# Cutting some output stores of an attention backward kernel at other rows

## The chip, the cores and the metric

The kernel runs on one core of one Trainium2 chip. A core has five engines with their own instruction streams: TensorE (PE, matmuls; its weight loads are listed as PEld), VectorE (DVE), ScalarE (ACT), GpSimd (POOL) and SyncE (SP). Data moves between the device memory (DRAM) and the on-chip buffer (SBUF) by DMA; 16 DMA engines serve the core. An instruction on SP or POOL only issues a transfer; the 16 DMA engines carry it out in packets, and each of the 16 adds one to a semaphore when its share of the transfer is done. Matmul results stand in PSUM, eight banks here.

The metric is the device time of one execution in microseconds (us), lower is better. The profile is one execution taken by the hardware profiler.

## The reference

Grouped-query attention with a softmax over all keys, its output, and the gradients for q, k and v:

```python
B, Hq, Hkv, Sq, Sk, D = 32, 32, 4, 4, 2048, 128      # all bfloat16
def _fwd_reference(q, k, v):
    k = jnp.repeat(k, Hq // Hkv, axis=1)
    v = jnp.repeat(v, Hq // Hkv, axis=1)
    scores = jnp.einsum("bhqd,bhkd->bhqk", q, k) * D ** -0.5
    return jnp.einsum("bhqk,bhkd->bhqd", _softmax(scores, axis=-1), v)

def reference(q, k, v, grad_out):
    out, vjp = jax.vjp(_fwd_reference, q, k, v)
    return (out, *vjp(grad_out))                      # out, dq, dk, dv
```

k and v are 64 MiB each and so are dk and dv; q, grad_out, out and dq are 1 MiB each. Nearly all traffic is k and v in, dk and dv out.

## The kernel before

One batch after another is worked through. The 32 query heads times 4 positions are the 128 rows of a tile; each of the 4 key heads has 2048 keys, held as 128 partitions of 16 keys (the index c, 16 blocks of 128). For a batch the kernel

- loads k and v, one transfer of 512 KB for each head (`LK`, line 154, and `LV`, line 160), issued from SP, into buffers `k_sb` (3 of them, each a whole batch) and `v_sb` (2),
- transposes k and v on PE, eight 128x128 blocks at a time (`KT`, `VT`, line 181), and copies the result out of PSUM on DVE (line 183),
- forms the scores (line 198), their maximum (line 211) and exponentials (line 222), the row sums (`NRM`), then transposes the exponentials (line 248) and gathers the output o (`O`, line 264),
- forms dP, dS and its transpose, and dq (`dQ`, line 264),
- forms dV and dK as eight outer products each (`outer`, matmuls in line 307, copies out of PSUM on ACT in line 311) into a 2 MB buffer out of a pool of four that dV and dK share.

The order on all engines is written out by hand (`HEAD`, `STEADY`, `TAIL`): one turn of the steady part mixes work of batch b with dK and dq of batch b-1 and with transposes of batch b+1, and issues the loads of batch b+2. A load of k waits until the dq of the batch that used the buffer has read it (three k buffers).

All results are stored from POOL's queue (`store`), in the order in which the program issues them: dq (line 294), dk and dv (line 337; the last batch in halves, line 323), o for two batches at a time (line 280). POOL also loads the next four batches' q and grad_out (line 142) every fourth batch. A store of dv or dk is one transfer of 128 partition rows by 4 heads of 4 KB, 2 MB in all, except:

- for every fourth batch (`b % 4 == 3`, b = 3, 7, ..., 27) dv goes out as heads 0 and 1 whole (128 rows) and heads 2 and 3 in a piece of 120 rows and a piece of 8 rows; the small piece goes first where b is 3, 11, 19 or 27, last where it is 7, 15 or 23,
- o of every second pair of batches (b = 7, 11, ..., 31) goes out as 52 rows and 76 rows (line 279).

Of the kernel before, what the change touches and what calls it, by code (L numbers as in the profile page):

```python
# [81 lines left out]
def kernel(ctx: ExitStack, tc: tile.TileContext, q, k, v, grad_out, out_0, out_1, out_2, out_3):  # L82
# [3 lines left out]
    P = 128  # L86
# [172 lines left out]
    def gathered(S, xt, kv):  # L259
        t = banks.take(1)  # L260
        ps = banks.ap(t)[:, 0, 0:D]
        for c in range(C):
            for h in range(NH):
                nc.tensor.matmul(  # L264
                    ps[G * h:G * h + G, :], lhsT=S[f"{xt}{c // 8}"][:, c % 8, G * h:G * h + G], rhs=S[kv][:, h, c, :],
                    start=(c == 0), stop=(c == C - 1), tile_position=(0, G * h),
                )
        return t, ps

    def O(b):  # L270
        S = st[b]
        t, ps = gathered(S, "et", "v")
        if b % 2 == 0:
            st["o"] = io_pool.tile([P, 2, D], BF16, name="o_sb")
        o_sb = st["o"][:, b % 2, :]
        nc.vector.tensor_scalar(out=o_sb, in0=ps, scalar1=S["rinv"][:], scalar2=None, op0=ALU.mult)
        banks.give(t)
        if b % 2:
            for r in (slice(0, 52), slice(52, P)) if b % 4 == 3 and b > 3 else (slice(0, P),):
                store.dma_start(out=o_f[b - 1:b + 1, r].rearrange("w p d -> p w d"), in_=st["o"][r])  # L280
        junk = sm_pool.tile([P, D], BF16, name="junk")
        S["delta"] = sm_pool.tile([P, 1], FP32, name="delta")
        nc.vector.tensor_tensor_reduce(
            out=junk[:], in0=o_sb, in1=S["do"], scale=1.0, scalar=0.0,
            op0=ALU.mult, op1=ALU.add, accum_out=S["delta"][:],
        )
# [9 lines left out]
    def outer(S, x, y, dst, name, i, b, copy):  # L296

        if name not in S:
            S[name + "left"] = 8
            S[name] = out_pool.tile([P, NH, C, D], BF16, name=name, tag="outp")  # L300
        t = banks.take(2)
        ps = banks.ap(t).rearrange("p a (j c d) -> p a j c d", j=2, c=2)
        for c in range(2):
            u = P * ((2 * i + c) % 8)
            for a in range(2):
                r = slice(2 * G * a, 2 * G * a + 2 * G)
                nc.tensor.matmul(  # L307
                    ps[:, a, :, c, :], lhsT=S[f"{x}{i // 4}"][r, u:u + P], rhs=S[y][r, :, :],
                    start=True, stop=True, tile_position=(2 * G * a, 0),
                )  # L310
        copy(  # L311
            out=S[name][:, :, 2 * i:2 * i + 2, :].rearrange("p h c d -> p h (c d)"),
            in_=banks.ap(t).rearrange("p a (j w) -> p (a j) w", j=2),
        )
        banks.give(t)
        S[name + "left"] -= 1
        if b == B - 1:

            half = f"{name}half{i // 4}"
            S[half] = S.get(half, 4) - 1  # L320
            if S[half] == 0:
                c = slice(8 * (i // 4), 8 * (i // 4) + 8)
                store.dma_start(
                    out=dst[b].rearrange("p h (c d) -> p h c d", d=D)[:, :, c, :].rearrange("p h c d -> p h (c d)"),
                    in_=S[name][:, :, c, :].rearrange("p h c d -> p h (c d)"),
                )
        elif S[name + "left"] == 0:
            o = S.pop(name)[:].rearrange("p h c d -> p h (c d)")
            parts = [(slice(0, P), slice(0, NH))]
            if name == "dv" and b % 4 == 3:  # L330

                cut = [(slice(0, 120), slice(2, 4)), (slice(120, P), slice(2, 4))]
                parts = [(slice(0, P), slice(0, 2))] + (cut if b % 8 == 7 else cut[::-1])
            for r, h in parts:
                store.dma_start(out=dst[b][r, h, :], in_=o[r, h])  # L337

    def dV(b, i, copy=nc.scalar.copy):
        outer(st[b], "e", "dop", dv_v, "dv", i, b, copy)  # L340

    def dK(b, i, copy=nc.scalar.copy):
        outer(st[b], "ds", "qp", dk_v, "dk", i, b, copy)

    def dP(b, i):
# [6 lines left out]
        banks.give(t)  # L352

    table = {"LK": LK, "LV": LV, "QDT": QDT, "O": O, "dQ": dQ, "NRM": NRM}
    for i, c in enumerate("ab"):
        for n, f in (("S", S_), ("EX", EX), ("dP", dP), ("ET", ET), ("dST", dST)):
# [16 lines left out]
    with tc.manual_schedule():  # L373

        for w in HEAD.split():
            w, b = w.split("@")
# [5 lines left out]
        for w in TAIL.split():  # L382
            w, b = w.split("@")
# [31 lines left out]
```

## Time and profile before

| | |
|---|---|
| median of 3 runs | 700.01 us (698.55 to 701.41) |
| the profiled execution | 700.94 us, its span 699.2 us |
| granted TensorE clock | 0.984 |
| busy share PE, DVE, ACT, POOL | 89%, 84%, 81%, 39% |
| moved by DMA | 274.45 MB, 393 GB/s over the span |

The span runs from the first to the last instruction that the profile shows. Busy shares are averages over the span; what bounds a stage is read from the chain of waits in that stage. In the profile the transfers issued from POOL stand under queue q0 (software dynamic), those from SP under q1 (hardware dynamic), and fetches of instructions under q8 and q14. An issue row gives the size of each transfer and the median time from its issue until the last of the 16 engines has reported its share.

### The profile page before, as it was taken

To read this page: it belongs to the slowest core of one execution; us is meant where nothing else is said; L and a number is where in the kernel's file an instruction comes from. 1 tells how busy PE (TensorE), PEld (TensorE's weight loads), DVE (VectorE), ACT (ScalarE), POOL (GpSimd) and SP (SyncE) were. 2 spreads that over 40 slices of the span, in tenths; PEclk is the share of its full clock that TensorE was granted. 3 is DMA by queue.
4 is the path that set the end of the run, shared out by engine and by line. 5 is a ranking of instruction groups with operands and counts; after the bars stand their busy time and mean duration, and the time that the engine had idled before them with its cause. 6 is when DMAs were issued, how large, how long until landed. Compare 5 with 4: busy or idle time off the path is not lost.

```text
span 699.2 us, 27997 instructions
## 1 busy us (share of the span) xinstructions
PE 625.1 (89%) x12352; PEld 452.5 (65%) x12352; DVE 586.6 (84%) x992; ACT 569.0 (81%) x673; POOL 270.8 (39%) x449
## 2 busy tenths in 40 slices
PE   6899999999988989989899888899988999888981
PEld 5577776667676666666566665667666667656661
DVE  5998999989887998879988888788888988878960
ACT  0698989889887888869798878887887988778994
POOL 1354342445342254432444423444333534314352
PEclk9999999999999999999999999999999999999996
DMA  8989999999999999999999999999999999999767
GB/s 341 394 305 411 417 415 416 416 412 417 413 415 414 413 416 409 414 405 403 417 395 410 412 407 398 381 413 413 418 399 371 414 412 416 397 385 375 291 253 276
DMA packets 74969, 274.45 MB, mean 393 GB/s; under 512 B 8033, under 2 KB 8061, under 8 KB 74848
## 3 DMA queue, kind: packets, MB, share of 16 engines
q0 software_dynamic: 36928, 138.17, 49.4%
q1 hardware_dynamic: 37920, 134.50, 48.6%
q8 instruction: 96, 1.57, 0.8%
q14 instruction: 25, 0.20, 0.1%
HBM read 136.31 MB, written 136.31 MB: 390 GB/s over the span
## 4 chain that ended last, share of the span: by engine, by line
DMA 48%; PE 41%; DVE 3%; issue 3%; ACT 2%; POOL 1%; SPq 0%; POOLq 0%; ACTq 0%; DVEq 0%
DMA k_sb<-in_k_dram 47%; PE banks L181 18%; PE banks L307 10%; PE banks L264 6%; PE banks L248 3%; PE banks L198 3%; ACT dv L311 1%; DVE kt L183 1%; DMA v_sb<-in_v_dram 1%; DVE ds L349 1%; DVE m L211 1%; DVE vt L183 0%; ACT dk L311 0%; PE banks L171 0%; POOL dop L231 0%
## 5 line engine op out<-in xcount | busy, mean ns | idle before, releaser
L311 ACT CAST dk<-banks 128x1024 bf16<-128x1024 f32 x256 | 251.0, 1027 | 44.0 <-PE banks L307 41.3
L311 ACT CAST dv<-banks 128x1024 bf16<-128x1024 f32 x256 | 245.7, 1028 | 46.2 <-PE banks L307 45.6
L183 DVE COPY kt<-banks 128x1024 bf16<-128x1024 bf16 x256 | 166.1, 683 | 19.5 <-PE banks L181 19.2
L181 PE MATMUL banks<-ident,k_sb 128*128 128x128 bf16 x2048 | 151.1, 224 | 31.9 <-DMA k_sb<-in_k_dram 24.1
L231 POOL TENSOR_SCALAR dop<-do_sb,rinv 32x128 bf16<-32x128 bf16 x128 | 76.6, 598 | 242.4 <-DVE rinv L239 139.5
L183 DVE COPY vt<-banks 128x1024 bf16<-128x1024 bf16 x256 | 166.3, 682 | 1.4 <-PE banks L181 1.2
L181 PEld LDWEIGHTS <-k_sb 128*128 128x128 bf16 x2048 | 123.3, 100 | 62.4 <-issue 34.4
L181 PE MATMUL banks<-ident,v_sb 128*128 128x128 bf16 x2048 | 142.4, 219 | 11.9 <-ACT dv L311 10.0
L181 PEld LDWEIGHTS <-v_sb 128*128 128x128 bf16 x2048 | 121.3, 98 | 24.5 <-issue 20.5
L307 PE MATMUL banks<-dop,e 64*128 64x256 bf16 x1024 | 98.5, 274 | 7.2 <-issue 4.5
L349 DVE SCALAR_TENSOR_TENSOR ds<-banks,delta,e 128x1024 bf16<-128x1024 f32 x64 | 82.2, 1284 | 18.2 <-PE banks L198 17.9
L337 POOL DMA_DIRECT2D out_dram<-dv x45 | 32.5, 724 | 151.5 <-ACT dv L311 147.5
L307 PE MATMUL banks<-qp,ds 64*128 64x256 bf16 x1024 | 85.6, 272 | 2.1 <-ACT dk L311 1.4
L231 POOL TENSOR_SCALAR qp<-q_sb,srinv 32x128 bf16<-32x128 bf16 x128 | 77.5, 605 | 10.6
L222 ACT ACTIVATE e<-banks,negb 128x1024 bf16<-128x1024 f32 x64 | 70.7, 1109 | 11.8 <-DVE negb L214 11.7
L211 DVE TENSOR_REDUCE m<-banks 128x1 f32<-128x1024 f32 x64 | 75.2, 1217 | 1.2 <-PE banks L198 1.2
L250 DVE COPY et<-banks 128x1024 bf16<-128x1024 bf16 x64 | 41.4, 686 | 36.0 <-PE banks L248 36.0
L307 PEld LDWEIGHTS <-e 64*128 64x128 bf16 x1024 | 33.8, 94 | 54.0 <-issue 37.1
L307 PEld LDWEIGHTS <-ds 64*128 64x128 bf16 x1024 | 41.2, 94 | 29.3 <-ACT dv L311 12.7
L250 DVE COPY dst<-banks 128x1024 bf16<-128x1024 bf16 x64 | 43.6, 682 | 1.8 <-PE banks L248 1.8
L198 PE MATMUL banks<-vt,qdt 128*32 128x512 bf16 x512 | 41.3, 388 | 0.7 <-issue 0.5
L198 PE MATMUL banks<-kt,qdt 128*32 128x512 bf16 x512 | 39.3, 384 | 0.9 <-DVE vt L183 0.3
(39 smaller groups left out, 461.6 us busy)
## 6 DMA issues: line engine op xcount, KB each, us to landing
k_sb<-in_k_dram SPq DMA_DIRECT2D x128, 512.0 KB, 16.6
v_sb<-in_v_dram SPq DMA_DIRECT2D x128, 512.0 KB, 20.8
out_dram<-dk POOLq DMA_DIRECT2D x31, 2048.0 KB, 24.1
out_dram<-dv POOLq DMA_DIRECT2D x24, 2048.0 KB, 27.6
out_dram<-dv POOLq DMA_DIRECT2D x9, 1024.0 KB, 23.0
out_dram<-dv POOLq DMA_DIRECT2D x7, 960.0 KB, 28.3
out_dram<-dk POOLq DMA_DIRECT2D x2, 1024.0 KB, 5.6
out_dram<-dq_sb POOLq DMA_DIRECT2D x32, 32.0 KB, 14.6
```

The lines of the kernel that those rows point to most:

```text
L181: nc.tensor.transpose(out=ps[:, 4 * hh + j, :], in_=S[which][:, 2 * (i % 2) + hh, 4 * (i // 2) + j, :], identity=ident[:])
L183: nc.vector.tensor_copy(out=S[f"{which}t{i}"][:], in_=ps)
L198: nc.tensor.matmul(ps[G * h:G * h + G, a, :], lhsT=S["qdt"][:, col, G * h:G * h + G], rhs=xt[:, 4 * (h % 2):4 * (h % 2) + 4, :].rearrange( ...
L211: nc.vector.reduce_max(out=S["m"][:, i:i + 1], in_=S[f"s{i}"][1], axis=AX.X)
L222: nc.scalar.activation(out=S[f"e{i}"][:], in_=ps, func=ACT.Exp, bias=S["negb"][:], scale=scale, accum_out=S["l"][:, i:i + 1],)
L231: nc.gpsimd.tensor_scalar(out=t[r, h % 2, :], in0=src[r, :], scalar1=by[r, :], scalar2=None, op0=ALU.mult)
L250: nc.vector.tensor_copy(out=S[f"{name}{i}"][:], in_=ps)
L264: nc.tensor.matmul(ps[G * h:G * h + G, :], lhsT=S[f"{xt}{c // 8}"][:, c % 8, G * h:G * h + G], rhs=S[kv][:, h, c, :], start=(c == 0), stop ...
L307: nc.tensor.matmul(ps[:, a, :, c, :], lhsT=S[f"{x}{i // 4}"][r, u:u + P], rhs=S[y][r, :, :], start=True, stop=True, tile_position=(2 * G * ...
L311: copy(out=S[name][:, :, 2 * i:2 * i + 2, :].rearrange("p h c d -> p h (c d)"), in_=banks.ap(t).rearrange("p a (j w) -> p (a j) w", j=2),)
L337: store.dma_start(out=dst[b][r, h, :], in_=o[r, h])
L349: nc.vector.scalar_tensor_tensor(out=S[f"ds{i}"][:], in0=ps, scalar=S["delta"][:], in1=S[f"e{i}"][:], op0=ALU.subtract, op1=ALU.mult,)
```

## The change

The three sets of split stores are cut elsewhere. The bytes stored and their addresses are the same as before.

- dv of b = 3, 7, ..., 27: head 0 whole (128 rows), then heads 1 to 3 in 120 rows and in 8 rows, always in this order.
- dv of b = 0, before one transfer: heads 0 and 1 whole, then heads 2 and 3 in 88 rows and in 40 rows.
- o of b = 7, 11, ..., 31: 104 rows and 24 rows.

```diff
         if b % 2:
-            for r in (slice(0, 52), slice(52, P)) if b % 4 == 3 and b > 3 else (slice(0, P),):
+            for r in (slice(0, 104), slice(104, P)) if b % 4 == 3 and b > 3 else (slice(0, P),):
                 store.dma_start(out=o_f[b - 1:b + 1, r].rearrange("w p d -> p w d"), in_=st["o"][r])
...
             parts = [(slice(0, P), slice(0, NH))]
-            if name == "dv" and b % 4 == 3:
-                cut = [(slice(0, 120), slice(2, 4)), (slice(120, P), slice(2, 4))]
-                parts = [(slice(0, P), slice(0, 2))] + (cut if b % 8 == 7 else cut[::-1])
+            if name == "dv" and b == 0:
+                parts = [(slice(0, P), slice(0, 2)), (slice(0, 88), slice(2, 4)), (slice(88, P), slice(2, 4))]
+            elif name == "dv" and b % 4 == 3:
+                parts = [(slice(0, P), slice(0, 1)), (slice(0, 120), slice(1, 4)), (slice(120, P), slice(1, 4))]
             for r, h in parts:
                 store.dma_start(out=dst[b][r, h, :], in_=o[r, h])
```

On POOL this makes two transfers more (both for dv of batch 0); all other instructions and their order on every engine are unchanged.

## The prediction

> **What bounds the kernel now.** I read the page first: engine shares, DMA slices, chain.
>
> ```profile
> PE 625.1 (89%) x12352; PEld 452.5 (65%) x12352; DVE 586.6 (84%) x992; ACT 569.0 (81%) x673; POOL 270.8 (39%) x449
> DMA packets 74969, 274.45 MB, mean 393 GB/s; under 512 B 8033, under 2 KB 8061, under 8 KB 74848
> q0 software_dynamic: 36928, 138.17, 49.4%
> q1 hardware_dynamic: 37920, 134.50, 48.6%
> DMA 48%; PE 41%; DVE 3%; issue 3%; ACT 2%; POOL 1%; SPq 0%; POOLq 0%; ACTq 0%; DVEq 0%
> DMA k_sb<-in_k_dram 47%; PE banks L181 18%; PE banks L307 10%; PE banks L264 6%; PE banks L248 3%; PE banks L198 3%; ACT dv L311 1%; DVE kt L183 1%; DMA v_sb<-in_v_dram 1%; DVE ds L349 1%; DVE m L211 1%; DVE vt L183 0%; ACT dk L311 0%; PE banks L171 0%; POOL dop L231 0%
> ```
>
> Both DMA queues together fill 98% of the 16 engines' span, and 47% of the chain is the landing of k. The chain in order of time shows where:
>
> ```profile
> 160.66 16.02 DMA k_sb<-in_k_dram
> ...
> 329.82 17.41 DMA k_sb<-in_k_dram
> ...
> 349.98 1.01 PE banks L264 x64
> ...
> 351.41 16.85 DMA k_sb<-in_k_dram
> ...
> 372.44 17.08 DMA k_sb<-in_k_dram
> ...
> 393.70 17.75 DMA k_sb<-in_k_dram
> ...
> 415.64 17.52 DMA k_sb<-in_k_dram
> ...
> 585.81 17.50 DMA k_sb<-in_k_dram
> ```
>
> Before 160.66 us the chain runs through PE; from there to 603.3 us (585.81 + 17.50) it is a loop: k lands, PE transposes it and does dq (line 264), dq frees a k buffer, the next k is issued. One turn is 85.8 / 4 = 21.45 us (415.64 − 329.82, four turns).
>
> The stages by engine (first row: the stage before the loop tells) and PE's waits for loads:
>
> ```profile
> core 0: us, PE busy (x) PEld busy (x) DVE busy (x) ACT busy (x) POOL busy (x), PEclk, DMA share, GB/s
> 100.00:200.00 100.00, 94.95 (x1862) 68.54 (x1862) 90.63 (x155) 87.45 (x105) 41.07 (x67) 1.00 1.03 415
> 200.00:300.00 100.00, 92.74 (x1864) 66.67 (x1862) 86.73 (x147) 84.96 (x100) 43.19 (x70) 0.98 1.03 414
> 300.00:600.00 300.00, 273.44 (x5421) 197.02 (x5419) 257.73 (x436) 249.88 (x295) 118.78 (x193) 0.99 1.02 405
> ```
> ```profile
> PE banks L181 <- DMA k_sb<-in_k_dram: 24.1, 21, 2.2
> PEld L181 <- DMA v_sb<-in_v_dram: 3.4, 16, 0.2
> ```
>
> DMA moves 415 GB/s at first and 405 GB/s from 300 to 600 us, while k is late: some of the 16 engines idle and some don't. So I asked which. The 16 completion steps of a transfer, worked out from the semaphore updates in the trace (us; o of batch 15 in 52 and 76 rows, of batch 19 in 76, dv of batch 19 in 8, dv of batch 3 in 8 and then 120):
>
> ```
> transfer        issued   1st     2nd     8th     15th    16th
> o 52 rows       336.94  347.99  348.16  350.33  352.06  360.85
> o 76 rows       337.60  348.43  348.56  351.16  352.83  361.68
> o 76 rows       423.18  433.35  433.67  436.16  437.11  447.92
> dv 8 rows       429.07  436.78  437.47  439.25  439.99  453.72
> dv 8 rows        93.95  104.06  104.09  106.88  108.03  108.87
> dv 120 rows      94.52  106.73  108.72  111.79  113.78  113.81
> ```
>
> From batch 15 on one engine is 9 to 14 us behind the other fifteen. Every load needs all 16, so that engine paces the loop. It is not the engine that the 120-row store spares: that one reports that store first (106.73, two us ahead of the second), without having been spared before.
>
> **Where the late engine sits.** How a split store is laid out shows in packet sizes. Single packets in windows of 1 ns (a mean of 32 GB/s is 32 bytes), at 360.126 us (the same row comes at 350.185 and 351.097), at 361.006 and at 447.280 us (the third row also comes at 436.239):
>
> ```profile
> DMA packets 1, 0.00 MB, mean 32 GB/s; under 512 B 1, under 2 KB 1, under 8 KB 1
> DMA packets 1, 0.00 MB, mean 1536 GB/s; under 512 B 0, under 2 KB 1, under 8 KB 1
> DMA packets 1, 0.00 MB, mean 24 GB/s; under 512 B 1, under 2 KB 1, under 8 KB 1
> ```
>
> The page has 8061 − 8033 = 28 packets between 512 B and 2 KB: seven 76-row stores on four engines, 19 rows each (38 pieces of 256 B = 4096 + 4096 + 1536 B). An engine without a share moves 4 B for each piece: 32 B for 52 rows, 24 B at the end of 76. This reading (a store takes the largest number of engines up to 16 that divides its rows, and starts on the engine after the last one that the split store before it used) gives exactly q0's 36,928 packets. Counting engines from the one that the first split store starts on as position 0, before spares position 7 in every 120-row store; positions 4, 5, 6 have no share of the 52 rows in batches 7, 15, 23 but one of the 76, and none of the 76 in batches 11, 19, 27. The late engine's 32-byte packet (360.126, nine us after the other two), its 1536-byte packet (361.006) and its 24-byte packet (447.280, 11 us after the one at 436.239) put it at position 4, 5 or 6. The trace does not tell which.
>
> [...]
>
> **The change part by part.**
>
> Placement. By the same rule, dv of batch 0 takes positions 0–10 (88 rows) and 11–15, 0–4 (40 rows); the next split starts at 5. Each 120-row piece then lies on 5–15 and 0–3 and spares position 4; 8 rows go to 4–11; 104 rows on 13 engines and 24 on 12 bring the start back to 5. So position 4 is spared in all seven, by three heads instead of two.
>
> If position 4 is the late engine: per four batches it now has 256 packets of 4 KB for loads and some 262 for stores, 85.8 us / 518 = 165.6 ns each; the fifteen move at 16 × 4096 B / 415 GB/s = 158 ns. Its dv in the split batch falls from 33 packets (16 + 16 + one of the 8 rows on average) to 11 (8 + 0 + 3): 22 × 165.6 ns = 3.6 us less, 82.2 us. The others get 1.5 more: (518 + 1.5) × 158 ns = 82.1 us. So it catches up: 3.6 of 85.8 us, 4.2%.
>
> What of this reaches the end: the loop lasts 603.3 − 160.7 = 442.6 us, so 18.6 us at most (4.2%). At least the lost rate: (415 − 405)/415 of 300 us = 7.2 us. Between them stands PE: 94.95% busy before the loop tells, 91.1% from 300 to 600, which is 11.4 us, and 2.2 us from 200 to 300: 13.6 us, within the 24.1 us that PE waits for k. Once k is in time, ACT (87.45%) and DVE (90.63%) are next, as in 100 to 200 us. I take 12.5 us, the PE reading less one us for waits that stay.
>
> First dv: positions 0–4 carry 24 packets for two heads' 16, 8 × 158 ns = 1.3 us later; no k piece is on the chain before 160 us, so nothing. Without that cover 1.3 us.
>
> POOL's queue: two more issues.
>
> ```profile
> L337 POOL DMA_DIRECT2D out_dram<-dv x45 | 32.5, 724 | 151.5 <-ACT dv L311 147.5 <-ACT dk L311 4.1
> ```
>
> 2 × 0.72 = 1.4 us on an engine idle 61%; behind them in the queue stands batch 1's `dop` for dV, some us off. Zero, at worst 1.4 us. The o pieces and the dv pieces as they stand:
>
> ```profile
> out_dram<-dv POOLq DMA_DIRECT2D x7, 960.0 KB, 28.3
> out_dram<-dv POOLq DMA_DIRECT2D x7, 64.0 KB, 26.0
> out_dram<-o_sb POOLq DMA_DIRECT2D x7, 38.0 KB, 24.1
> out_dram<-o_sb POOLq DMA_DIRECT2D x7, 26.0 KB, 23.9
> ```
>
> Of o, 38 and 26 KB become 52 and 12 KB, some 4 KB an engine on average either way: zero, at worst one packet of 158 ns a store. The dv pieces become 1440 and 96 KB; nothing in the loop waits for a store's landing as long as four output buffers cover it (28.3 us against two turns of 21.45), and the cover remains.
>
> Sum: 700.94 (profiled execution, span 699.2) − 12.5 = 688.4. That execution is 0.93 us over the median of 700.01, so 687.5 to 688.4; I say 688.
>
> **Rivals.**
>
> Late engine at position 5 or 6: it isn't spared. It gets 7 × 3 packets of the 8-row pieces instead of 8 and one fewer of o: 12 more in all by the same count (2113 for 2101), 12 × 165.6 ns = 2.0 us, on the loop in full: 702 to 703 us. For it: the three positions look alike in this trace. Against it: of 16 places the change spares one of just these three, where a place chosen blindly would do so three times in 16. It decides as soon as the late engine is not position 4.
>
> Position 7 becomes a second late engine: it gets 118 packets more, 118 × 165.6 ns = 19.5 us of work if it is as slow, only its being spared hid it, and both then lag: 703 to 706. Against it: 106.73 us, ahead of all before its first relief. [...]
>
> Next-late engines take over: the fifteenth step trails the first by 4 to 7 us too (348.43 to 352.83). If these lie 1% behind, little is won: 3 to 4 us, 697. For it: at 350 us half of the engines are two us or more behind the first (8th step 350.33 against 347.99).
>
> **Numbers.** Position 4: 0.58, 688 us with its own range 682 to 695. Position 5 or 6: 0.22. Position 7: 0.10. Next-late: 0.10. What tells from no change is 0.5%, 3.5 us. Faster: 0.58 and 0.03 of the next-late case, 0.61. Slower: 0.10 of position 5 or 6 and 0.07 of position 7, 0.17. Same: the rest, 0.22. The range 682 to 704 leaves out a gain over 18 us and the upper half of the position 7 case, under 0.2.
>
> **What would show it.** Right: q0 at 36,976 packets and 8081 under 512 B (the placement as counted), k's pieces of the chain shorter than 16 us or fewer after 200 us, 413 GB/s or more from 300 to 600 us, PE's wait for k under 12 us, the sixteenth step within 5 us of the fifteenth. Wrong: k pieces of 17 us and 405 GB/s as before, with one engine 10 us late; then the late engine is not at position 4. If the loads are in time and the span is the same, the loop was not paced by them.

## The result and the profile after

The changed kernel takes 688.3 us (median, 686.99 to 694.1), the kernel before on the same chip 700.16 us (698.55 to 701.98): a ratio of 0.984, 95% interval 0.981 to 0.988. The profiled execution took 688.33 us (its span is 686.5 us). That is 12.6 us less than the 700.94 us from which the sum was made.

The page of the kernel after, busy shares, queues and chain:

```profile
PE 621.9 (91%) x12352; PEld 450.2 (66%) x12352; DVE 584.8 (85%) x992; ACT 569.1 (83%) x673; POOL 269.9 (39%) x451
DMA packets 75017, 274.44 MB, mean 400 GB/s; under 512 B 8081, under 2 KB 8165, under 8 KB 74896
q0 software_dynamic: 36976, 138.16, 50.3%
q1 hardware_dynamic: 37920, 134.50, 48.8%
PE 54%; DMA 33%; DVE 4%; issue 3%; ACT 2%; POOL 2%; SPq 0%; POOLq 0%; ACTq 0%; DVEq 0%
```

PE does the same work, and the same bytes move at 400 in place of 393 GB/s. PE's busy time is 3.2 us shorter for the same 12352 matmuls, and the granted TensorE clock of the profiled execution is 0.990 where it was 0.984. In the executions of the kernels below it is 0.975 to 0.989 where position 4 isn't relieved and 0.987 to 0.994 with two heads. So the clock tends to go with the relief; whether a part of the gain is the clock's own, no run separates. The chain was 48% DMA and 41% PE; it is 33% and 54%. In the chain in order of time, the landings of k:

```profile
200.66 15.97 DMA k_sb<-in_k_dram
220.81 17.62 DMA k_sb<-in_k_dram
...
283.49 17.36 DMA k_sb<-in_k_dram
...
493.08 17.01 DMA k_sb<-in_k_dram
...
597.24 15.87 DMA k_sb<-in_k_dram
617.29 18.34 DMA k_sb<-in_k_dram
```

The first of them now stands at 200.66 us, not at 160.66, and there are 13 of them where before had 19. One is no shorter than it was (16 to 18 us); there are stretches between them in which k is in time.

The stages of after by engine (the same columns as before: window; length, then busy us of PE, PEld, DVE, ACT, POOL; clock, DMA share, GB/s), and of before the one row that the prediction doesn't show:

```profile
100.00:200.00 100.00, 96.70 (x1965) 70.20 (x1954) 91.50 (x157) 89.16 (x106) 40.80 (x67) 1.00 1.02 411
200.00:300.00 100.00, 93.96 (x1846) 67.70 (x1834) 88.75 (x150) 86.30 (x103) 43.02 (x70) 0.98 1.03 415
300.00:600.00 300.00, 278.42 (x5565) 201.25 (x5566) 261.29 (x447) 254.90 (x301) 119.97 (x198) 1.00 1.03 413
600.00:650.00 50.00, 45.75 (x931) 32.12 (x928) 43.62 (x75) 42.09 (x51) 18.86 (x31) 1.00 0.99 395
```
```profile
600.00:650.00 50.00, 43.38 (x832) 31.64 (x828) 40.29 (x70) 38.39 (x48) 15.15 (x26) 0.97 1.00 384
```

From 300 to 600 us DMA moves 413 GB/s where it moved 405, and PE is busy 278.42 us where it was 273.44. PE's waits for loads in after (total, times, mean):

```profile
PE banks L181 <- DMA k_sb<-in_k_dram: 15.6, 15, 2.2
PEld L181 <- DMA v_sb<-in_v_dram: 1.9, 7, 0.6
```

24.1 us have become 15.6, not nothing. Where the time is won shows in the issues of dk's stores, of batches 8, 13, 27 and 30; first before, then after (start, duration):

```profile
208.04 0.76 POOL L337 DMA_DIRECT2D out_dram<-dk  x1
...
315.76 0.76 POOL L337 DMA_DIRECT2D out_dram<-dk  x1 [0.31 <-ACT dk L311]
...
613.66 0.78 POOL L337 DMA_DIRECT2D out_dram<-dk  x1
...
676.27 0.76 POOL L337 DMA_DIRECT2D out_dram<-dk  x1 [0.59 <-ACT dk L311]
```
```profile
207.56 0.76 POOL L338 DMA_DIRECT2D out_dram<-dk  x1
...
311.17 0.76 POOL L338 DMA_DIRECT2D out_dram<-dk  x1
...
603.42 0.79 POOL L338 DMA_DIRECT2D out_dram<-dk  x1
...
663.77 0.76 POOL L338 DMA_DIRECT2D out_dram<-dk  x1 [0.39 <-ACT dk L311]
```

After is ahead by 0.5, 4.6, 10.2 and 12.5 us: next to nothing up to batch 8, and from there 0.55 us a batch on average (12.0 us over 22 batches), though not evenly: 0.8 us a batch up to batch 13, 0.4 up to 27, 0.75 behind that. One batch takes 21.28 us before and 20.74 us after ((676.27 − 208.04) / 22 and (663.77 − 207.56) / 22).

The comparisons leave out disturbed runs, and in the two kernels with four heads (below) these are the profiled ones and, in one of the two, all but one, so that no row of their profiles is read.

The 16 completion steps say the same. Worked out from the semaphore updates, a mean over all k and v loads issued from 300 to 600 us, in us behind the first step (the last five columns of kernels belong to the experiments below):

```
step    before  after   no splits  one head  half  two heads  two, small piece first
8th       2.6     5.6      1.3        1.9     3.6      9.3         9.4
12th      3.4     7.3      2.1        2.7     4.8     10.2        10.7
15th      5.4     8.7      3.3        3.8     6.7     10.9        11.5
16th     13.9    11.5     14.0       14.3    13.2     11.4        11.9
```

In before one engine ends 8.5 us after the fifteenth, so that a load that fifteen engines have finished stands waiting for one. In after the last ends 2.8 us after the fifteenth, and several others are late with it.

The last engine of the profiled execution of after isn't the one of before. The page of after has 8165 − 8081 = 84 packets between 512 B and 2 KB, twelve for each of the seven 24-row stores: 12 engines have a share of those rows, four pieces of 256 B each, and four have none. By the placement as the prediction reads it, position 4 now has a share of both pieces of every split o. Positions 5 to 8 alone, which get the most packets in after, have none of the 24 rows: they send a 16-byte packet in place of a share (four pieces of 4 B). From 300 to 600 us the last packet of a split o is such a 16-byte one in three rounds of three, at 354.452, 437.689 and 522.283 us, 1.0 to 1.9 us behind the last packet of an engine with a share. This row answers for 1 ns at each of the three times:

```profile
DMA packets 1, 0.00 MB, mean 16 GB/s; under 512 B 1, under 2 KB 1, under 8 KB 1
```

In another profiled execution of this kernel (685.97 us) the 16-byte packets aren't the last, so which engine takes over is not the same every time.

### The profile page after: what moved, and what is told of

It is laid out like the page before. It is cut to its first block, busy times and chain, and to the rows that moved or that the text cites. A ratio compares the mean times of both kernels' runs of the same rounds, so it can differ in the third digit from the quotient of the medians.

```text
span 686.5 us, 28002 instructions
## 1 busy us (share of the span) xinstructions
PE 621.9 (91%) x12352; PEld 450.2 (66%) x12352; DVE 584.8 (85%) x992; ACT 569.1 (83%) x673; POOL 269.9 (39%) x451
## 2 busy tenths in 40 slices
DMA packets 75017, 274.44 MB, mean 400 GB/s; under 512 B 8081, under 2 KB 8165, under 8 KB 74896
## 3 DMA queue, kind: packets, MB, share of 16 engines
q0 software_dynamic: 36976, 138.16, 50.3%
## 4 chain that ended last, share of the span: by engine, by line
PE 54%; DMA 33%; DVE 4%; issue 3%; ACT 2%; POOL 2%; SPq 0%; POOLq 0%; ACTq 0%; DVEq 0%
DMA k_sb<-in_k_dram 33%; PE banks L181 23%; PE banks L307 14%; PE banks L264 7%; PE banks L198 5%; PE banks L248 5%; ACT dv L311 2%; DVE kt L183 1%; DVE ds L350 1%; POOL dop L231 1%; DVE m L211 1%; DVE vt L183 1%; PE banks L171 1%; POOL out_dram L323 0%; POOL qp L231 0%
## 5 line engine op out<-in xcount | busy, mean ns | idle before, releaser
L181 PE MATMUL banks<-ident,k_sb 128*128 128x128 bf16 x2048 | 147.9, 222 | 21.5 <-DMA k_sb<-in_k_dram 15.6
L181 PEld LDWEIGHTS <-k_sb 128*128 128x128 bf16 x2048 | 121.2, 99 | 51.3 <-issue 32.2
```

What stands on the lines that cost most here:

```text
L181: nc.tensor.transpose(out=ps[:, 4 * hh + j, :], in_=S[which][:, 2 * (i % 2) + hh, 4 * (i // 2) + j, :], identity=ident[:])
```

## Experiments

All kernels are the changed one with the edit shown. The theory: one engine, at position 4 counted from the start of the first split store, is slower than the others; a packet taken from it there is time won; nothing else in the change matters. The rivals: the gain comes from the number or shape of the transfers; another position would do as well; the engine relieved before, position 7, is the slow one. The placement is the prediction's reading throughout. How many engines share a piece shows in the packets (36,928 and 36,976 on q0 in before and after, both as counted, and the 28 and 84 packets between 512 B and 2 KB). On which engine a piece starts (the cursor, by that reading one engine further than the last of the split store before) no packet shows, as the trace names no engine: it is the author's reading, borne out, but for the kernel with one head (below), by the times when the start is moved (688.3 us where it spares position 4, 702.0 to 705.5 where 5, 7 or 15) and by the sizes of the late packets where these were read.

In what follows a position's load is the number of 4 KB packets that this placement gives it in POOL's queue over the whole run; the mean of all positions is about 2092, and position 4 has 2101 in before and 1953 in after. The loads from SP's queue, 256 of 512 KB, make 32,768 packets of 4 KB; taken as shared alike by the 16 engines, that adds 2048 to every position.

### No split, the same splits without a place, and other places

No split at all:

```diff
-            if name == "dv" and b == 0:
+            if False:
...
-            elif name == "dv" and b % 4 == 3:
+            elif False:
...
-            for r in (slice(0, 104), slice(104, P)) if b % 4 == 3 and b > 3 else (slice(0, P),):
+            for r in (slice(0, P),):
```

> No store is split (dv and o of every batch whole). Theory (one DMA engine, at position 4, is slower in the mixed stage; splits matter only by what they take off it): position 4 carries 2092 packets of 4 KB in the store queue against 2101 before and 1953 in the changed kernel, so about the time before, 697 to 702 us, with one engine 10 us behind the others at late loads. Rival 1 (position 7 is slow too and its relief in the kernel before was worth something): clearly slower than before, 706 us or more. Rival 2 (the split stores of before only cost time): as fast as the changed kernel, 688 us.

The first dV not cut, so that all later ones start elsewhere (position 15 is spared):

```diff
-            if name == "dv" and b == 0:
+            if False:
```

> The changed kernel without the split of the first dv: the 120-row pieces then spare position 15 instead of 4, by the same three heads. Theory (position 4 is the late one): the gain is gone, 699 to 703 us (position 4 carries 2106 packets). Rival (the gain comes from three heads instead of two, fewer changes of order, or the other cut of o, wherever they lie): 688 us.

The first dV cut at row 100 (position 7 is spared), and at row 108 (position 5):

```diff
-                parts = [(slice(0, P), slice(0, 2)), (slice(0, 88), slice(2, 4)), (slice(88, P), slice(2, 4))]
+                parts = [(slice(0, P), slice(0, 2)), (slice(0, 100), slice(2, 4)), (slice(100, P), slice(2, 4))]
```

> First dv cut at 100 rows: everything as in the changed kernel, but position 7 is spared, as before, now by three heads. Theory: 699 to 703 us. Rival (the amount matters, not the place): 688 us. Rival (the first dv's cut brings the gain by itself): 688 us.

> First dv cut at 108 rows: position 5, the neighbour, is spared. Theory (position 4 alone is late): 699 to 703 us. Rival (the late engine is at position 5 and position 4 merely shares something with it): as fast as or faster than the changed kernel, 688 us or less. [...]

All stores cut as often as in the change, but in halves of 64 rows, which by the same placement lie on all 16 engines and spare none:

```diff
-                parts = [(slice(0, P), slice(0, 2)), (slice(0, 88), slice(2, 4)), (slice(88, P), slice(2, 4))]
+                parts = [(slice(0, P), slice(0, 2)), (slice(0, 64), slice(2, 4)), (slice(64, P), slice(2, 4))]
...
-                parts = [(slice(0, P), slice(0, 1)), (slice(0, 120), slice(1, 4)), (slice(120, P), slice(1, 4))]
+                parts = [(slice(0, P), slice(0, 1)), (slice(0, 64), slice(1, 4)), (slice(64, P), slice(1, 4))]
...
-            for r in (slice(0, 104), slice(104, P)) if b % 4 == 3 and b > 3 else (slice(0, P),):
+            for r in (slice(0, 64), slice(64, P)) if b % 4 == 3 and b > 3 else (slice(0, P),):
```

> Control: the same transfers in the same number as the changed kernel, but each cut at 64 rows, so that every piece lies on all 16 engines and none is spared. Theory: as with no split at all, 700 to 704 us. Rival (smaller stores or the earlier landing of a first part bring the gain): 688 us.

Measured, each against the kernel before on the same chip (medians 700.0 us for equal halves, 700.2 for after, and 699.5 for the other four, which ran on one further chip):

| spared | median, us | ratio (95%) |
|---|---|---|
| nothing, no splits | 702.2 | 1.003 (1.001 to 1.005) |
| nothing, equal halves | 701.6 | 1.002 (1.001 to 1.003) |
| position 15 | 705.5 | 1.008 (1.006 to 1.010) |
| position 7 | 702.6 | 1.004 (1.002 to 1.007) |
| position 5 | 702.0 | 1.003 (1.001 to 1.006) |
| position 4 (after) | 688.3 | 0.984 (0.981 to 0.988) |

The kernels that spare positions 7 and 5 differ from after in nothing but the row at which the first dV is cut, and take 14.3 and 13.7 us more, on a chip whose before is 0.6 us faster. So it is the place, and of the places tried only position 4. Equal halves, with the same issues on POOL, cost 1.5 us (0.6 to 2.3). Sparing position 7 with three heads is worth nothing against no splits at all (702.6 and 702.2), so before's relief went to an engine that didn't need it. Position 15 came out above the range expected, the kernel without splits at its upper end; with position 15 spared, position 4 gets 2106 packets against 2092 without splits, 14 x 165.6 ns = 2.3 us, and 3.3 were measured.

That the late engine sits where it was put by the sizes shows in the position 15 kernel, too. There, by the same placement, 104 rows lie on positions 7 to 15 and 0 to 3, and positions 4, 5 and 6 send a 64-byte packet (16 pieces of 4 B) in place of their share. Three such packets go out for each store. The latest of each three, at 362.757, 449.590 and 535.128 us, came 10 us after the other two (at 352.3 and 352.8, 437.3 and 439.2, 523.9 and 524.9):

```profile
DMA packets 1, 0.00 MB, mean 64 GB/s; under 512 B 1, under 2 KB 1, under 8 KB 1
```

Three windows of 1 ns answer with this same row. So on this chip, too, the late engine is at position 4, 5 or 6. Position 5 is spared on the same chip and nothing is won. The trace of that kernel rules out position 6: there, counted the same way, positions 6 to 9 have no share of the 24 rows and send 16-byte packets, and the late packet is one of 1024 bytes, an engine's share of the 24 rows. It comes at 359.263, 446.093 and 532.602 us, 5 to 9 us after all others of its size, while the four 16-byte packets of its round are out by 354.2, 437.2 and 522.2 us. The row at each of the three times:

```profile
DMA packets 1, 0.00 MB, mean 1024 GB/s; under 512 B 0, under 2 KB 1, under 8 KB 1
```

What is left is position 4, and on other chips sparing it wins 12 us and more.

In the run without splits the steps of the stores alone would mislead: their sixteenth is but 3 us behind the fifteenth. The loads show the engine (14.0 against 3.3 us in the table above).

### How much relief

Two heads in place of three, and one head:

```diff
-                parts = [(slice(0, P), slice(0, 1)), (slice(0, 120), slice(1, 4)), (slice(120, P), slice(1, 4))]
+                parts = [(slice(0, P), slice(0, 2)), (slice(0, 120), slice(2, 4)), (slice(120, P), slice(2, 4))]
```

> Position 4 is spared by two heads, 14 packets in each split batch; this is the amount that the kernel before spared at position 7. Theory: on the line, 693 us (690 to 695). Rival (three heads were needed for all of the gain): 698 us or more. Rival (two are as good as three, the rest of the gain is bounded by the other fifteen engines): 688 us.

```diff
-                parts = [(slice(0, P), slice(0, 1)), (slice(0, 120), slice(1, 4)), (slice(120, P), slice(1, 4))]
+                parts = [(slice(0, P), slice(0, 3)), (slice(0, 120), slice(3, 4)), (slice(120, P), slice(3, 4))]
```

> As the changed kernel, but position 4 is spared by one head (7 packets of 4 KB in each split batch instead of 21). Theory (the time follows what the late engine has to carry, until it has caught up at about 22 packets): from 702 us with nothing spared to 688 us with 21 packets a straight line gives 697 us (695 to 700). Rival (any relief of position 4 suffices, because only its order in the ring matters): 688 us.

All four heads:

```diff
-                parts = [(slice(0, P), slice(0, 1)), (slice(0, 120), slice(1, 4)), (slice(120, P), slice(1, 4))]
+                parts = [(slice(0, 120), slice(0, 4)), (slice(120, P), slice(0, 4))]
```

> Position 4 is spared by four heads, 28 packets in each split batch, and the first piece of one whole head falls away. Theory (balanced at about 22): the other fifteen bound the time, 687 to 690 us, no more gain. Rival (the late engine is still the last with three heads): 684 us by the line.

Measured: two heads 686.9 us, a ratio of 0.981 (0.978 to 0.983), 6 us better than expected and no worse than three. One head 703.4 us, 1.005 (1.003 to 1.007): a miss, with no gain at all where 3 us were expected. Four heads, where 687 to 690 us were expected: 692.0, 702.9, 706.1 and 706.6 us in four executions. There is no ratio, so this form stays undecided.

**Why one head wins nothing.** The packet counts of one head fit the placement as exactly as those of before and after do (36,752 packets on q0, as counted). The times of the odd packets don't. Placed so, position 4 has a share of both pieces of every split o, and its packets for the 24 rows (1024 bytes) would be the late ones each time. In the trace of the one-head kernel, windows of 1 ns at 360.362, 446.900 and 532.967 us, each 8.5 to 10 us after the packet of its size before it:

```profile
DMA packets 1, 0.00 MB, mean 64 GB/s; under 512 B 1, under 2 KB 1, under 8 KB 1
...
DMA packets 1, 0.00 MB, mean 1024 GB/s; under 512 B 0, under 2 KB 1, under 8 KB 1
...
DMA packets 1, 0.00 MB, mean 16 GB/s; under 512 B 1, under 2 KB 1, under 8 KB 1
```

The late engine has no share of the 104 rows in the first of these rounds, one of both pieces in the second, and none of the 24 rows in the third; in the fourth (619.026 us) it is again one with both. It cannot have changed: one engine alone ends 10 us after all others, 14.3 against 3.8 us in the loads. So the start of the splits moves on, from round to round. If the two pieces of dV leave it where it is, the 13 and 12 engines of the two pieces of o move it by 25, which is 9 modulo 16. Position 4, counted from the start of o in steps of 9, then has offsets 13, 4, 11 and 2: outside the 104 rows (offsets 13 to 15), in both (0 to 8), outside the 24 rows (9 to 12), in both. That is the order seen. A store of one head of 120 rows is therefore not placed as one of two or three heads is, though its packets are as many as the same placement gives. On which engines it lies wasn't shown.

What was meant as a small dose was thus, by its time (703.4 us), no dose at position 4. A proper one: two heads, but in every eighth dV alone, and every fourth pair of o:

```diff
-            elif name == "dv" and b % 4 == 3:
-                parts = [(slice(0, P), slice(0, 1)), (slice(0, 120), slice(1, 4)), (slice(120, P), slice(1, 4))]
+            elif name == "dv" and b % 8 == 7:
+                parts = [(slice(0, P), slice(0, 2)), (slice(0, 120), slice(2, 4)), (slice(120, P), slice(2, 4))]
...
-            for r in (slice(0, 104), slice(104, P)) if b % 4 == 3 and b > 3 else (slice(0, P),):
+            for r in (slice(0, 104), slice(104, P)) if b % 8 == 7 and b > 7 else (slice(0, P),):
```

> Two heads are cut in every eighth dv alone, and every fourth pair of o: position 4 is spared 34 packets in all (2058 against a mean of 2092), where two heads in every fourth dv spare 90 and gain 13.1 us. If the gain goes with the packets taken off position 4, it is 34/90 of that, 5 us: 695 us (692 to 698). If nothing is won until position 4 has stopped being the last, it is 700 to 703 us, with one engine alone 9 us or more behind as before.

Two heads in every fourth dV, but with the 8-row piece first and the first dV cut at row 30, which by the same placement keeps position 4 the spared one and puts the 8-row pieces on other engines; the same with all four heads; and the changed kernel again, all on one chip:

```diff
-                parts = [(slice(0, P), slice(0, 2)), (slice(0, 88), slice(2, 4)), (slice(88, P), slice(2, 4))]
+                parts = [(slice(0, P), slice(0, 2)), (slice(0, 30), slice(2, 4)), (slice(30, P), slice(2, 4))]
...
-                parts = [(slice(0, P), slice(0, 1)), (slice(0, 120), slice(1, 4)), (slice(120, P), slice(1, 4))]
+                parts = [(slice(0, P), slice(0, 2)), (slice(120, P), slice(2, 4)), (slice(0, 120), slice(2, 4))]
```

> First dv cut at 30 and 98 rows, then every fourth dv two heads whole and two in 8 rows (stored first) and 120 rows. By the placement rule the spared position stays 4 (1996 packets of about 2092), but the 8-row pieces lie on positions 13 to 15 and 0 to 3 in place of 5 to 11. If only the relief of position 4 counts, the time is that of the two heads without the move, 685 to 688 us. If the 8-row pieces hurt where they lay before, it is shorter, 682 to 685. If the rule of the cursor is wrong for the new first cut, position 4 isn't spared and it is 700 to 705.

> All four heads in 8 rows (stored first) and 120 rows, first dv cut at 30 and 98 rows: position 4 gets 1898 packets, and the 28 extra ones that four heads give to seven engines lie on positions 13 to 15 and 0 to 3. If four heads in the order 120 and 8 were slow because those extra packets fell on an engine at 5 to 8 that is next to late, this is 686 to 691 us. If more than three heads is too much whatever engine gets the rest, it is 700 us or more, with one engine of positions 13 to 3 as the late one.

> The changed kernel again, beside the two-head version on the same chip: 687 to 690 us by its runs so far. If two heads with the 8-row pieces elsewhere are better than three, this is 2 to 5 us longer than that one; if the number of heads beyond two makes no difference, they are within 1.5 us.

| cut | packets at position 4 | median, us | ratio (95%) | won, us |
|---|---|---|---|---|
| equal halves | 2085 (all alike) | 701.6 | 1.002 (1.001 to 1.003) | −1.5 |
| two heads, every eighth | 2058 | 695.5 | 0.994 (0.992 to 0.996) | 4.5 |
| two heads | 2002 | 686.9 | 0.981 (0.978 to 0.983) | 13.1 |
| two heads, small piece first | 1996 | 685.5 | 0.978 (0.975 to 0.981) | 14.6 |
| three heads (after, again) | 1953 | 689.2 | 0.984 (0.981 to 0.988) | 10.8 |
| four heads, small piece first | 1898 | 691.2 | 0.987 (0.983 to 0.991) | 8.8 |

Won is against before on the same chip. The half dose came out at 695.5 us, where 695 stood. 34 packets off the mean win 4.5 us, 90 win 13.1, 96 win 14.6: 0.13 to 0.15 us a packet. Before itself is faster than the kernels without relief, so this is the low reading; two heads against equal halves, on one chip, are 14.7 us for 83 packets (2085 and 2002), 0.18 us a packet. Then it turns: 139 off win 10.8 and 194 win 8.8 (at 691.2 us, where 686 to 691 were expected). The windows from 300 to 600 us of the one-head, the half-dose and the small-piece-first kernel:

```profile
300.00:600.00 300.00, 271.93 (x5372) 197.04 (x5372) 254.20 (x431) 245.70 (x292) 115.65 (x191) 0.98 1.02 402
```
```profile
300.00:600.00 300.00, 275.18 (x5449) 198.76 (x5446) 260.35 (x443) 251.09 (x299) 113.83 (x188) 0.99 1.02 408
```
```profile
300.00:600.00 300.00, 280.69 (x5631) 203.10 (x5628) 261.53 (x446) 255.78 (x303) 121.56 (x201) 0.99 1.03 415
```

402, 408 and 415 GB/s: the last is what DMA moved before the loop told in the kernel before. PE's waits for k in the same three:

```profile
PE banks L181 <- DMA k_sb<-in_k_dram: 30.3, 22, 2.3
```
```profile
PE banks L181 <- DMA k_sb<-in_k_dram: 25.2, 20, 2.3
```
```profile
PE banks L181 <- DMA k_sb<-in_k_dram: 13.8, 13, 2.2
```

With the matched relief the sixteenth step of the loads is 0.5 and 0.4 us behind the fifteenth, and 1.2 us behind the twelfth (table of steps, two heads both ways): no engine is alone any more. From the eighth step to the sixteenth nine engines end within 2.5 us, at 415 GB/s, and PE still waits 13.8 us for k. The other seven end earlier (the seventh step, which the table doesn't show, is at 4.4 and 5.8 us), so the load isn't even yet; what evening it out would win wasn't tried.

Two heads with the small piece first is the best kernel of these. On the same chip it takes 683.75 to 685.91 us, the changed kernel 685.69 to 692.12: 3.8 us between the medians, with ranges that just touch. Against two heads without the move (0.978 and 0.981, with intervals that overlap) nothing is shown for the place of the 8-row piece.

## Why the prediction was right, point by point

**The loop and its pacemaker.** As put: k's landing paces the loop, one engine paces k, and the place of the 120-row pieces decides whether that engine is relieved. The experiments with other places show it, and that position 4, one of the three that the trace of before allowed, is the one. That it would be 4 and not 5 or 6 the prediction took from the aim of the change (0.58 against 0.22), not from a trace of the kernel before.

**The placement.** 36,976 packets on q0 and 8081 under 512 B, as counted. The start that the reading gives fits the times of the runs with two or three heads in a piece (685.5 to 689.2 us with position 4 spared in every fourth batch, 702.0 to 705.5 with another position); the one-head run (36,752 packets on q0 as counted, 703.4 us) shows that a right count doesn't prove a right place.

**"So it catches up: 3.6 of 85.8 us."** Right for position 4, wrong for the loop. It was 21.28 to 20.74 us a batch, 2.5%, where 4.2% was the most it could be. Two things in the step were off. The lag of the late engine was taken too large: 165.6 against 158 ns is 4.8%, or 22 of its 518 packets in four batches. The two-head runs show that 14 of the 518 are enough, about 3%. Part of it is the four turns that the 85.8 us were taken from: 21.45 us each, where the mean is 21.28. And the step took the other fifteen as a block that gets 1.5 packets more. With three heads position 4 has 139 packets fewer than the mean, 40 to 50 more than the two-head runs; what is over goes to the others, and unevenly: positions 5 to 8 get 2113, positions 12 to 15 2084. Two heads, which were the right dose, won 1 to 4 us more by the medians.

**The term of 12.5 us.** 12.6 measured between the profiled executions, but not by the way it was read. The prediction let PE return to its rate of before the loop, 94.95%, from 300 to 600 us, for 11.4 us there and 2.2 before. PE came back to 92.8% (278.42 of 300 us) alone, and 5.6 us were won between batches 13 and 27 (10.2 − 4.6). The rest lies outside that window: 4.1 us between batches 8 and 13, 2.3 us after batch 27. One term was too large, one too small and one missing, and they cancelled: that the sum came within 0.1 us is luck, though its range and its direction are not.

**The costs put at nothing.** Two more issues on POOL are there, and cheap:

```profile
L338 POOL DMA_DIRECT2D out_dram<-dv x47 | 33.2, 710 | 147.5 <-ACT dv L311 141.0
```

0.7 us more busy on an engine that is idle 61%. All issues and cuts together without any relief (equal halves) are 1.5 us over the kernel before (0.6 to 2.3).

**The signs.** Fewer k pieces on the chain after 200 us, 413 GB/s, the packets, and the sixteenth step within 5 us of the fifteenth: all as put (13 for 19; 413; 2.8 us in the loads). PE's wait for k under 12 us was missed, at 15.6; even the best kernel has 13.8. The prediction took that wait as the late engine's alone, and more than half of it stays when no engine is alone any more.

**The rivals.** Positions 5 and 6 fall: 5 because it was spared and nothing was won, 6 by the sizes of the late packets in that same kernel. Position 7 as a second slow engine falls: relieved alone, it wins nothing (702.6 us, 702.2 without splits), and burdened with more (2113 in after) it doesn't stop the gain (688.3 us). The next-late engines do take over, as the last rival had it (in the profiled execution of after one at positions 5 to 8), but at 2.5% and not at 1%.

**Left open.** Before is 1 to 3 us faster than the kernels without relief, though its position 4 has as many packets as theirs or more (2101; 2092 without splits, 2100 and 2098 with positions 7 and 5 spared); why isn't known. What four heads run into isn't settled: the runs fit an overload of the engines that get the 8-row pieces, but none separates it. A kernel that spares position 6 alone wasn't run; the traces speak against it.

## What to carry to other kernels

When a load waits for all 16 engines, compare the fifteenth with the sixteenth completion step of the loads, not of the stores alone: here a gap that stayed (8.5 us on average in before) showed that one engine was the pacemaker. Fewer or more transfers alone didn't help here (702.2 us without splits, 701.6 in equal halves). A split of a few stores so that it skips that engine did, by 0.13 to 0.18 us for each packet taken off (about one packet's time, 0.166 us by the prediction's estimate), up to about 3% here (14 of 518 packets in four batches) and not beyond. The place was found by trying it, in a kernel that differs in nothing but the start: one position out of the four tried was worth some 14 us, and its neighbour nothing.

## What the runs showed of the hardware that was not expected

- A store of one head (120 rows of 4 KB) is laid on the engines otherwise than a store of two or three heads with the same rows: its packets are as many as counted (36,752 on q0), but, as the late packets read, the start of the next split doesn't move with it (they come at 360.362, 446.900 and 532.967 us on engines with three different shares).
- One engine of 16 was slower than the others, by about 3% as estimated from the dose below, at position 4, as counted, on each of the three chips that the experiments ran on: by the late packets on one, by the gain from sparing it on the two others. It ended 8.5 us after the fifteenth step in the loads of before. With 14 of some 518 packets fewer in every four batches (90 and 96 in all, of 2092 in POOL's queue and 2048 in SP's) the last step was 0.5 and 0.4 us behind the fifteenth.
- The gain turns at that dose: 0.978 at 96 packets, 0.984 at 139, 0.987 at 194. Times with too much relief also spread more, 685.69 to 692.12 us for three heads against 683.75 to 685.91 for two.
